# Retention followed by a routed mixture of experts: the due slots of the tail tokens and of the expert weights are changed

## Chip, cores and metric

One NeuronCore of a Trainium2 chip runs the whole kernel. The metric is the device time of one execution in microseconds (us); lower is better. The kernel before has a median of 495.64 us over 14 runs (493.08 to 499.93).

## What is computed

The first half is a decayed attention without softmax: 8 batches, 8 heads, 576 positions, head size 64. Its output, 4608 tokens of 512 numbers, goes to a mixture of 8 experts. Each token takes the two experts with the highest noisy logits and adds their weighted results.

```python
scores = q @ k.T / sqrt(64)
x = (scores * gamma[h] ** (pos_q - pos_k), causal) @ v
logits = x @ w_gate + log1p(exp(x @ w_noise)) * noise
top2, weights = two largest of logits, softmax over the two
out[token] = sum over its two experts e of weight * (relu(x @ w1[e]) @ w2[e])
```

The inputs are float32. The matmuls run in bfloat16.

## The kernel before

**First half: slots.** The attention is cut into 16 units, numbered u = 0 to 15: two batches (a pair, `bp`), four heads (`hq`), one batch of the pair (`b`). A loop over n = 0 to 16 (line 1178) works on them in a software pipeline; one pass of it is called slot n here. The instruction order on each engine is the order of the Python text (`tc.manual_schedule`), so an instruction that has to wait holds everything behind it on its engine. In slot n:

- SyncE (SP) issues the loads of unit n+4: `raw_q`, `raw_k`, `raw_v` (lines 170 and 175), four buffers each. In slots 2, 6 and 10 it also issues the loads of the next tail (line 182).
- TensorE (PE) computes scores of unit n (line 263), the output of unit n-1 (lines 313, 321), transposes q and k of unit n+1 (line 248) and sums states (line 287).
- GpSimd (POOL) casts k and q of unit n+2 with the decay factors: `kn` (line 199), `qb` (line 206).
- ScalarE (ACT) copies out of PSUM and casts: `xT` (327), `QT` and `KT` (250), `vn`, the cast of v of unit n+2 (189), `Tb` (293).
- VectorE (DVE) applies the causal mask to the scores (268).

**Tail tokens.** A unit covers 512 of the 576 positions. The remaining 64 positions of both batches of a pair and all heads are the tail of that pair. `cast_tail(bp)` casts them: q and k on POOL (`qt`, `kt`, line 217), v on ACT (`vt`, line 220). `tr_tail(bp)` transposes `qt` and `kt` on PE (line 229) and copies the result out on ACT (`TT`, line 232). The tail's own scores and output (lines 338 to 357, then `xT`, line 357) come in slots 4bp+2 and 4bp+4. The load buffers `rawt_q`, `rawt_k`, `rawt_v` exist once each. Before, the casts and transposes are placed at the end of these slots:

```python
if u % 4 == 2 and u < 12 or u == 1:
    at.cast_tail((u + 2) // 4)
if u % 4 == 3 and u < 15 or u == 1:
    at.tr_tail((u + 1) // 4)
```

That is: pair 0 cast and transposed in slot 1; pairs 1, 2 and 3 cast in slots 2, 6 and 10 and transposed in slots 3, 7 and 11.

**Router.** When a pair is complete (slots 4, 8, 12, 16) `route(bp)` is appended to a list, and its pieces are issued between the steps of the following slots: logits and rows (`xr`, lines 502 to 507), two table switches on ACT (`nl` 525 and `d` 574), the choice of two experts on DVE, list positions, the placement matrices `olo` and `oh` on DVE (665 to 672), and a store of the rows, `xd<-xr`, on SP (line 653). On POOL it has `pd` (579, 580, 625), `pl` (597 to 648) and the copies into `xr` (651) that the store waits for. In slots 11 to 14 POOL issues the weights of experts 0 and 1 (lines 1096 and 1099).

**Second half: tiles.** The expert stage has 35 tiles of 256 tokens, in order of their expert: two tiles of expert 0, three of expert 1, five of each later one (five more tiles were computed early, between the last slots). PE interleaves g2 of tile i (line 986, the second matmul) with g1 of tile i+1 (line 966, the first matmul, four pieces of 256 rows called fp 0 to 3). ACT takes relu of fp 0 and 2 (971), the copy `xgT` after fp 0 (953) and some of the scaled results `y` (1013); DVE takes relu of fp 1 and 3 (973) and the rest. The piece buffer `p1` has three places.

**Weights of experts 2 to 7.** Each expert has 8 parts of 512 KB. A part is loaded by SP into a staging tile `wst` (lines 902 and 905, four buffers) and cast by ACT into the expert's tile (line 916). Before, a pair of parts is loaded by `wload(i + 1)` at the end of tile i and cast by `wcast(i + 1)` at the end of tile i+1, four tiles for each expert: tiles 0 to 3 for expert 2, 4 to 7 for expert 3, and so on to 20 to 23 for expert 7. Three expert tiles exist, so expert e takes the place of expert e-3. Expert e is used from tile 5e-5.

Of the kernel before, what the change touches and what calls it, by code (L numbers as in the profile page):

```python
# [10 lines left out]
F32 = mybir.dt.float32  # L11
# [4 lines left out]
Act = mybir.ActivationFunctionType  # L16

P = 128
N = 4608
NCOL = N // P  # L20
E = 8
F = 1024
DM = 512
KD = DM // P
KF = F // P
TS = 256
NTE = 5
# [15 lines left out]
LATE = [(e, t) for e in range(E) for t in range(NTE) if (e, t) not in [x[1:] for x in EARLY]]  # L43
# [804 lines left out]
def experts(tc, K, wp, w1, w2, keep, xd, yd, out, W, pre):  # L848

    nc = tc.nc  # L850
# [3 lines left out]
    NT = len(LATE)  # L854
    order = {V.engine, nc.scalar.engine, nc.gpsimd.engine, nc.tensor.engine, nc.sync.engine}
    with tc.tile_pool(name="moe_g", bufs=1) as gp, \
# [14 lines left out]

        st = {}
        writes = []
        parts = {}

        def firsts(i):

# [5 lines left out]
            return [2 * t + s >= ONLYA[e] for s in range(2)]  # L883


        loads = {}
        i0 = -4
        for e in range(2, E):
            i0 = max(i0 + 4, LATE.index((e - 3, NTE - 1)) + 1 if e > 2 else 0)
            for j in range(4):  # L890
                loads[i0 + j] = e, j

        def wload(i):

            if i not in loads:
                return
            e, j = loads[i]
            parts[i] = []
            for k in (2 * j, 2 * j + 1):
                t = stg.tile([P, F], F32, name="wst")  # L900
                if k < KD:
                    nc.sync.dma_start(out=t, in_=w1[e, k * P:(k + 1) * P, :])
                else:
                    f = 2 * (k - KD)
                    nc.sync.dma_start(out=t.rearrange("p (fo d) -> p fo d", fo=2),
                                      in_=w2[e, f * P:(f + 2) * P, :].rearrange("(fo fi) d -> fi fo d", fi=P))
                parts[i].append((k, t))

        def wcast(i):
            if i not in parts:  # L910
                return
            e = loads[i][0]
            if e not in W:
                W[e] = (gp if e % 3 == 2 else wp).tile([P, KD * F + KF * DM], BF16, name=f"w{e % 3}")
            for k, t in parts.pop(i):
                nc.scalar.activation(W[e][:, k * F:(k + 1) * F], t, Act.Copy)  # L916

        def xgof(i):
            return pre[i] if i < len(pre) else xgs[i % NX]
# [120 lines left out]
        with tc.manual_schedule(engines=order):  # L1040
            for i in range(len(pre), 5):
                clear(xgs, i % NX)
                for s in range(2):
                    gather(tc, keep, xd, xgof(i), i, s)
            small(0)
            small(1)
            transp(0)()
            transp(1)()
            for _ in g1(0, {}):
                pass  # L1050
            small(2)
            small(3)
            wload(0)
            pv = 0
            for i in range(NT + 1):
                if i:
                    fin(i - 1)
                if i < NT:
                    ev = transp(i + 2)
                    cb = lambda: comb(i - 1)  # L1060
                    a = g1(i + 1, {0: ev, 1: cb}) if i + 1 < NT else iter(())
                    for _ in g2(i):
                        next(a, None)
                        next(a, None)
                    for _ in a:
                        pass
                    small(i + 4)
                if i + 1 >= NT:
                    comb(i - 1)

                if i + 5 < NT:
                    clear(xgs, (i + 5) % NX)
                for s in range(2):
                    if i + 5 < NT:
                        gather(tc, keep, xd, xgof(i + 5), i + 5, s)
                while pv <= i + 2 and stored(pv, i):
                    for s in range(2):
                        prev(pv, s)
                    pv += 1
                for s in range(2):  # L1080
                    if i and seconds(i - 1)[s]:
                        scat(i - 1, s)
                st.pop(i - 1, None)
                wcast(i)
                wload(i + 1)

        last = nc.gpsimd.tensor_copy(keep["nov2"], keep["nov"]).ins
        for w in writes:
# [15 lines left out]
def kernel(  # L1104
# [12 lines left out]
    nc = tc.nc  # L1117
# [10 lines left out]
    W = {}  # L1128
# [3 lines left out]
    with ExitStack() as actx, tc.manual_schedule(engines=order):  # L1132
        at = Attention(tc, actx, raw, None, q, k, v)
        at.load(0, (nc.scalar, nc.sync, nc.sync))
        for u in (1, 2, 3):
            at.load(u, (nc.sync,) * 3)
        at.load_tail(0, (nc.sync,) * 3)
        at.tables()
        K = at.K = constants(nc, cp)
        wg32 = at.bf.tile([P, KD, 2 * E], F32, name="wg32", bufs=1)  # L1140
        nc.scalar.dma_start(out=wg32[:, :, :E], in_=moe_w_gate.rearrange("(do di) e -> di do e", di=P))
        nc.scalar.dma_start(out=wg32[:, :, E:], in_=moe_w_noise.rearrange("(do di) e -> di do e", di=P))
        wgn = cp.tile([P, KD, 2, 2 * E], BF16, name="wgn")
        rt = Router(tc, actx, K, at, wgn, moe_noise, xd, keep)
        NU = 16
        pend = []
        routed = []

        work = []

        def more():
            while work and next(work[0], work) is work:
                work.pop(0)

        def piece():
            while pend and next(pend[0], pend) is pend:
                pend.pop(0)
                routed.append(0)

        def step():  # L1160
            piece()
            if n == NU:
                more()

        zero = at.cp.tile([P, DM], F32, name="zero")
        nc.gpsimd.memset(zero, 0.0)
        at.cast(0, nc.vector)
        nc.gpsimd.tensor_copy(wgn[:, :, 0], wg32)
        nc.gpsimd.tensor_tensor(wgn[:, :, 1], wg32, wgn[:, :, 0], Alu.subtract)
        at.tr(0, "q")  # L1170
        at.tr(0, "k")
        at.cast_v(0)
        for t in at.Tb:
            nc.vector.memset(t, 0.0)
        at.cast(1, nc.vector)
        at.cast_v(1)
        rt.fixed()
        for n in range(NU + 1):
            u, p = n, n - 1
            live, prev = u < NU, p >= 0  # L1180
            bp, hq, b = at.unit(p)
            tail = prev and b
            if u + 4 < NU:
                at.load(u + 4, (nc.sync,) * 3)
            if n % 4 == 2 and n // 4 < 3:
                at.load_tail(n // 4 + 1, (nc.sync,) * 3)
            if n == 1:
                rt.load_noise(nc.sync)
            if live:
                at.scores(u, 0)  # L1190
            step()
            if prev:
                at.out(p)
            step()
            if u + 1 < NU:
                at.tr(u + 1, "q")
            if n == NU - 2:
                more()
            step()
            if live:  # L1200
                at.scores(u, 1)
            step()
            if u + 2 < NU:
                at.cast(u + 2)
            if u + 1 < NU:
                at.tr(u + 1, "k")
            step()
            if tail:
                at.scores_tail(bp, hq)
            step()  # L1210
            if live:
                at.states(u)
            if tail:
                at.out_tail(bp, hq)
            if prev and p % 4 == 3:
                pend.append(rt.route(bp))
            step()
            if u % 4 == 2 and u < 12 or u == 1:
                at.cast_tail((u + 2) // 4)
            if u % 4 == 3 and u < 15 or u == 1:  # L1220
                at.tr_tail((u + 1) // 4)
            if n in (11, 12, 13, 14):
                load_weights(nc, wp, moe_w1, moe_w2, (n - 11) // 2, W, (n - 11) % 2)
            piece()
            if n == NU - 4:
                nc.sync.dma_start(out=yd[:P, :], in_=zero)

            if n == NU - 3:
                assert len(routed) >= 2
                work.append(early(tc, K, at, keep, xd, yd, W, EARLY, routed))  # L1230
            if n in (NU - 3, NU - 2):
                more()
        while pend:
            piece()
            step()
        rt.finish()

        for i in range(1):
            xg = raw.tile([P, 2, 4, P], F32, name="raw_q").rearrange("p c h w -> p (c h w)")[:, :2 * XW].rearrange(
                "p (s w) -> p s w", s=2)  # L1240
            nc.gpsimd.memset(xg, 0.0)
            for s in range(2):
                gather(tc, keep, xd, xg, i, s)
            pre.append(xg)
        rt.overflow_list()
        while work:
            more()
# [32 lines left out]
```

## Time and profile before

| what | value |
|---|---|
| median of 14 runs | 495.64 us |
| the profiled execution's own time | 496.0 us |
| its span, first to last instruction | 494.0 us |
| slots and early tiles | about 0 to 216 us |
| expert tiles | about 216 to 475 us |
| last scatter, overflow test, end | 475 to 494 us |
| PE busy, whole span | 412.1 us (83%) |
| ACT busy, whole span | 275.7 us (56%) |
| POOL busy, whole span | 274.6 us (56%) |
| DVE busy, whole span | 234.7 us (48%) |
| data moved | 104.18 MB, 211 GB/s on average |

The page divides the span into 40 slices of 12.35 us. A busy share over the whole span mixes the two halves, so it is read by stage. In a timeline row the columns are: start, duration, engine, line, operation, output<-input, shapes, count, and in square brackets the idle time before it with the releaser. SPq and PEq are sequencers: an SPq row is the time in which a DMA was issued, not the transfer itself.

### The profile page before, as it was taken

The page shows a single profiled execution, that of the slowest core. Times are in us where ns is not written, and L with a number is a line of the kernel's source. Part 1 is how long each engine was busy: PE and PEld are TensorE (multiplying, and loading weights), DVE is VectorE, ACT ScalarE, POOL GpSimd, SP SyncE. Part 2 cuts the span into 40 slices and gives each one's busy share as a digit, 9 for nine tenths or more (in the row PEclk, how much of TensorE's full clock was granted, in tenths as well). Part 3 has the DMA queues.
Part 4 walks back from the last instruction along what each step waited for, and adds up shares of the span by engine and source line. Part 5 has one row for each costly group of instructions (what it writes and reads, how often), then busy time and mean ns, then how long its engine had stood idle before and what let it go on. Part 6 is the DMA issues. An engine that isn't in the chain of part 4 may idle for free.

```text
span 494.0 us, 11741 instructions
## 1 busy us (share of the span) xinstructions
PE 412.1 (83%) x4688; PEld 299.9 (61%) x4688; DVE 234.7 (48%) x600; ACT 275.7 (56%) x405; POOL 274.6 (56%) x372
## 2 busy tenths in 40 slices
PE   1675378586877699989999999999999999999950
PEld 1464367464666567666766766666676676766630
DVE  3532066966866738724324434344344454454240
ACT  3681689678658467554665665755654643323200
POOL 5460735835954425585255717547567777776440
PEclk9977597989587799999999999999999999999995
DMA  8999993697795822574697887877978945545330
GB/s 243 285 257 215 269 295 55 205 304 168 205 219 130 173 63 97 175 261 154 217 307 213 278 306 222 317 263 246 349 251 275 343 140 194 169 142 186 112 128 2
DMA packets 92856, 104.18 MB, mean 211 GB/s; under 512 B 22135, under 2 KB 69752, under 8 KB 92800
## 3 DMA queue, kind: packets, MB, share of 16 engines
q1 hardware_dynamic: 77040, 70.04, 47.9%
q0 software_dynamic: 14176, 32.83, 23.3%
q8 instruction: 37, 0.61, 0.5%
q10 hardware_dynamic: 1584, 0.56, 0.4%
q14 instruction: 19, 0.16, 0.1%
HBM read 84.66 MB, written 28.72 MB: 230 GB/s over the span
## 4 chain that ended last, share of the span: by engine, by line
PE 58%; DMA 5%; DVE 4%; ACT 3%; SPq 2%; issue 1%; POOL 1%; POOLq 0%; ACTq 0%
PE p L966 25%; PE po L986 24%; DMA raw_v<-in_v_dram 3%; PE pt L950 3%; PE x L408 1%; SPq L182 1%; PE T L398 1%; PE S L398 1%; DVE olo L665 1%; SPq L175 1%; DVE oh L672 1%; DVE S L268 1%; DVE oh L669 1%; DMA rawt_v<-in_v_dram 1%; ACT xr L505 1%
## 5 line engine op out<-in xcount | busy, mean ns | idle before, releaser
L966 PE MATMUL p<-xgT,w 128*128 128x256 bf16 x1120 | 211.3, 273 | 0.0
L986 PE MATMUL po<-w,hT 128*128 128x512 bf16 x560 | 209.8, 379 | 0.0
L966 PEld LDWEIGHTS <-w 128*128 128x128 bf16 x1120 | 109.6, 98 | 70.3
L973 DVE TENSOR_SCALAR hT<-p 128x512 bf16<-128x512 f32 x70 | 48.4, 692 | 145.5 <-PE p L966 145.5
L971 ACT ACTIVATE hT<-p 128x512 bf16<-128x512 f32 x70 | 41.8, 597 | 119.9 <-PE p L966 94.9
L843 POOL DMA_INDIRECT xg<-xd,xi x68 | 68.9, 1013 | 20.2 <-issue 13.9
L1033 POOL DMA_INDIRECT out_dram<-o,ix x45 | 45.6, 1013 | 58.2 <-DVE o L1027 50.6
L268 DVE TENSOR_TENSOR S<-S,mask 128x1024 bf16<-128x1024 f32 x32 | 39.1, 1221 | 50.6 <-PE S L263 50.6
L995 POOL DMA_INDIRECT prv<-yd,ix x45 | 45.1, 1002 | 25.6 <-DMA yd<-y 12.3
L986 PEld LDWEIGHTS <-hT 128*128 128x128 bf16 x560 | 54.8, 98 | 7.5
L916 ACT ACTIVATE w<-wst 128x1024 bf16<-128x1024 f32 x48 | 47.9, 1048 | 0.0
L953 ACT ACTIVATE xgT<-pt 128x1024 bf16<-128x1024 bf16 x35 | 35.6, 1017 | 1.4 <-PE pt L950 1.4
L199 POOL TENSOR_TENSOR kn<-raw_k,kg 128x1024 bf16<-128x1024 f32 x14 | 26.7, 1904 | 15.0 <-DMA raw_k<-in_k_dram 6.1
L1027 DVE SCALAR_TENSOR_TENSOR o<-po,g,prv 128x512 f32<-128x512 f32 x45 | 31.6, 742 | 0.8 <-PE po L986 0.8
L263 PE MATMUL S<-QT,KT 64*64 64x128 bf16 x512 | 17.2, 269 | 17.5 <-ACT KT L250 8.9
L206 POOL TENSOR_TENSOR qb<-raw_q,qg 128x1024 bf16<-128x1024 f32 x14 | 26.7, 1904 | 0.0
L263 PEld LDWEIGHTS <-KT 64*64 64x64 bf16 x512 | 11.2, 132 | 22.0 <-issue 10.3
L250 ACT ACTIVATE QT<-tr 128x1024 bf16<-128x1024 bf16 x16 | 16.4, 1022 | 12.1 <-DMA raw_v<-in_v_dram 8.1
L293 ACT ACTIVATE Tb<-T 64x512 bf16<-64x512 f32 x32 | 18.9, 590 | 5.8 <-PE T L287 5.3
L950 PE MATMUL pt<-ident,xg 128*128 128x128 bf16 x272 | 20.7, 219 | 1.2 <-ACT xgT L953 1.2
L248 PE MATMUL tr<-ident,qb 128*128 128x128 bf16 x128 | 13.8, 271 | 9.5 <-DVE qb L206 9.5
L287 PE MATMUL T<-vn,kn 64*64 64x64 bf16 (+2 forms) x512 | 21.4, 221 | 0.0
(211 smaller groups left out, 593.2 us busy)
## 6 DMA issues: line engine op xcount, KB each, us to landing
wst<-in_moe_w_dram SPq DMA_DIRECT2D x48, 512.0 KB, 5.8
raw_k<-in_k_dram SPq DMA_DIRECT2D x32, 256.0 KB, 6.3
raw_v<-in_v_dram SPq DMA_DIRECT2D x32, 256.0 KB, 6.5
yd<-y SPq DMA_DIRECT2D x16, 512.0 KB, 3.7
raw_q<-in_q_dram SPq DMA_DIRECT2D x15, 512.0 KB, 6.4
xd<-xr SPq DMA_DIRECT2D x12, 396.0 KB, 4.0
w<-in_moe_w_dram POOLq DMA_DIRECT2D x4, 1024.0 KB, 11.9
yd<-raw_v SPq DMA_DIRECT2D x5, 512.0 KB, 4.0
```

What stands on the lines that cost most here:

```text
L268: nc.vector.tensor_tensor(S.rearrange("p h c r t -> p (h c) (r t)"), p.rearrange("p h (c r) t -> p (h c) (r t)", r=2), self.K["mask"].rear ...
L843: tc.nc.gpsimd.indirect_dma_start(out=xg[:, s, :], out_offset=None, in_=xd[:, :], in_offset=IOff(ap=keep["xi"][:, j:j + 1], axis=0), bound ...
L916: nc.scalar.activation(W[e][:, k * F:(k + 1) * F], t, Act.Copy)
L950: nc.tensor.transpose(pt[:, di, s * P:(s + 1) * P], xb[:, di * P:(di + 1) * P], K["ident"])
L953: return lambda: nc.scalar.activation(xgT, pt, Act.Copy)
L966: nc.tensor.matmul(p1[:, f2, :], lhsT=w[:, o:o + P], rhs=xgT[:, di, :], start=(di == 0), stop=(di == KD - 1))
L971: nc.scalar.activation(hT[:, 2 * fp:2 * fp + 2, :], p1, Act.Relu)
L973: V.tensor_relu(hT[:, 2 * fp:2 * fp + 2, :], p1)
L986: nc.tensor.matmul(po[s], lhsT=hT[:, fi, s * P:(s + 1) * P], rhs=w[:, o:o + DM], start=(fi == 0), stop=(fi == KF - 1))
L995: nc.gpsimd.indirect_dma_start(out=prv[i % NP][:, s, :], out_offset=None, in_=yd[:rows, :], in_offset=IOff(ap=st[i]["ix"][:, s, 1:2], axis=0),
L1027: V.scalar_tensor_tensor(o[:, s, :], st[i]["po"][s], st[i]["g"][:, s:s + 1], prv[i % NP][:, s, :], Alu.mult, Alu.add)
L1033: ins = nc.gpsimd.indirect_dma_start(out=out[:, :], out_offset=IOff(ap=st[i]["ix"][:, s, 0:1], axis=0), in_=st[i]["o"][:, s, :], in_offset ...
```

## The change

Two things are moved; no instruction of the computation is added or taken away.

1. **Tail tokens.** `cast_tail` of pairs 1, 2, 3 moves from the end of slots 2, 6, 10 to the end of slots 4, 8, 12. `tr_tail` moves from slots 3, 7, 11 to slots 5, 9, 13. Pair 0 stays in slot 1. The loads of the tails stay where they are on SP, in slots 2, 6 and 10.
2. **Expert weights.** Parts are now queued one by one. Three are loaded before tile 0; each cast is followed by the load of the next part. Casts are no longer at the end of a tile but inside g1: after fp 0 (behind the `xgT` copy) and after fp 2. Expert 2 still takes two casts in each of tiles 0 to 3. Experts 3 to 7 take 2, 1, 2, 1, 2 casts over five tiles, from tile 5e-11: tiles 4 to 8 for expert 3, up to 24 to 28 for expert 7.

```diff
-        parts = {}
+        parts = []
...
-        loads = {}
-        i0 = -4
+
+        casts = {}
         for e in range(2, E):
-            i0 = max(i0 + 4, LATE.index((e - 3, NTE - 1)) + 1 if e > 2 else 0)
-            for j in range(4):
-                loads[i0 + j] = e, j
-
-        def wload(i):
-
-            if i not in loads:
+            i0 = 5 * e - 11 if e > 2 else 0
+            assert e == 2 or i0 > LATE.index((e - 3, NTE - 1))
+            for j, c in enumerate((2, 1, 2, 1, 2) if e > 2 else (2, 2, 2, 2)):
+                casts[i0 + j] = c
+            assert i0 + j + 1 < LATE.index((e, 0))
+        queue = [(e, k) for e in range(2, E) for k in range(KD + KF // 2)]
+
+        def wload():
+
+            if not queue:
                 return
-            e, j = loads[i]
-            parts[i] = []
-            for k in (2 * j, 2 * j + 1):
-                t = stg.tile([P, F], F32, name="wst")
...
+            e, k = queue.pop(0)
+            t = stg.tile([P, F], F32, name="wst")
...
+            parts.append((e, k, t))
+
+        def wcast(i, j):
+
+            if j >= casts.get(i, 0):
                 return
-            e = loads[i][0]
+            e, k, t = parts.pop(0)
...
-            for k, t in parts.pop(i):
-                nc.scalar.activation(W[e][:, k * F:(k + 1) * F], t, Act.Copy)
+            nc.scalar.activation(W[e][:, k * F:(k + 1) * F], t, Act.Copy)
+            wload()
...
-            wload(0)
+            for _ in range(3):
+                wload()
...
-                    cb = lambda: comb(i - 1)
-                    a = g1(i + 1, {0: ev, 1: cb}) if i + 1 < NT else iter(())
+                    def first():
+                        ev()
+                        wcast(i, 0)
+                    a = g1(i + 1, {0: first, 1: lambda: comb(i - 1), 2: lambda: wcast(i, 1)}) if i + 1 < NT else iter(())
...
-                wcast(i)
-                wload(i + 1)
...
-            if u % 4 == 2 and u < 12 or u == 1:
-                at.cast_tail((u + 2) // 4)
-            if u % 4 == 3 and u < 15 or u == 1:
-                at.tr_tail((u + 1) // 4)
+            if n == 1 or n in (4, 8, 12):
+                at.cast_tail(n // 4)
+            if n % 4 == 1 and n < NU:
+                at.tr_tail(n // 4)
```

More of the change, by code (lines that the diff above doesn't have):

```diff
@@ L883, in seconds @@
             return [2 * t + s >= ONLYA[e] for s in range(2)]
-        loads = {}
-        i0 = -4
+        casts = {}
         for e in range(2, E):
-            i0 = max(i0 + 4, LATE.index((e - 3, NTE - 1)) + 1 if e > 2 else 0)
-            for j in range(4):
-                loads[i0 + j] = e, j
-        def wload(i):
-            if i not in loads:
-                return
-            e, j = loads[i]
-            parts[i] = []
-            for k in (2 * j, 2 * j + 1):
-                t = stg.tile([P, F], F32, name="wst")
[L901 to L910, printed above, removed]
+            i0 = 5 * e - 11 if e > 2 else 0
[6 more added lines that the diff above has]
+            if not queue:
+                return
+            e, k = queue.pop(0)
+            t = stg.tile([P, F], F32, name="wst")
+            if k < KD:
+                nc.sync.dma_start(out=t, in_=w1[e, k * P:(k + 1) * P, :])
+            else:
+                f = 2 * (k - KD)
+                nc.sync.dma_start(out=t.rearrange("p (fo d) -> p fo d", fo=2),
+                                  in_=w2[e, f * P:(f + 2) * P, :].rearrange("(fo fi) d -> fi fo d", fi=P))
+            parts.append((e, k, t))
+        def wcast(i, j):
+            if j >= casts.get(i, 0):
                 return
-            e = loads[i][0]
+            e, k, t = parts.pop(0)
             if e not in W:
                 W[e] = (gp if e % 3 == 2 else wp).tile([P, KD * F + KF * DM], BF16, name=f"w{e % 3}")
-            for k, t in parts.pop(i):
-                nc.scalar.activation(W[e][:, k * F:(k + 1) * F], t, Act.Copy)
+            nc.scalar.activation(W[e][:, k * F:(k + 1) * F], t, Act.Copy)
+            wload()
         def xgof(i):
```

## The prediction

> **What bounds the kernel now.** I read the stages first, then the waits, then the timelines of ACT, PE and SP around the longest wait. The table of stages (columns: PE, PEld, DVE, ACT, POOL busy us with counts, granted PE clock, DMA share, GB/s):
>
> ```profile
> 37.00:54.00 17.00, 6.78 (x150) 5.39 (x145) 2.67 (x3) 2.08 (x5) 3.46 (x4) 0.67 1.05 213
> 54.00:77.00 23.00, 16.55 (x370) 13.77 (x370) 11.04 (x27) 21.43 (x30) 11.27 (x9) 0.72 1.11 278
> 77.00:90.00 13.00, 9.90 (x213) 8.05 (x210) 9.65 (x27) 10.79 (x17) 8.95 (x19) 0.87 0.11 22
> ...
> 216.00:475.00 259.00, 257.77 (x1955) 179.57 (x1955) 111.89 (x296) 133.40 (x178) 157.05 (x158) 1.00 0.70 235
> ```
>
> The expert stage is PE alone: 257.77 of 259 us busy at full clock. Nothing off PE shortens it. The slots (0 to 216) have holes: from 37 to 54 ACT did 2.08 us of work. The list of waits (us in total, times, longest) names the cause:
>
> ```profile
> ACT vt L220 <- DMA rawt_v<-in_v_dram: 17.7, 3, 14.6
> ...
> POOL qt L217 <- DMA rawt_q<-in_q_dram: 13.5, 2, 13.2
> ...
> PE tr L229 <- ACT QT L250: 12.0, 1, 12.0
> ```
>
> and the timelines show it in place, ACT first, then PE, then SP:
>
> ```profile
> 38.87 0.38 ACT L357 ACTIVATE xT<-x 128x256 bf16<-128x256 f32 x1
> 53.85 0.63 ACT L220 ACTIVATE vt<-rawt_v 128x512 bf16<-128x512 f32 x1 [14.59 <-DMA rawt_v<-in_v_dram]
> 54.38 1.07 ACT L327 ACTIVATE xT<-x 128x512 bf16<-128x512 f32 x2
> ```
>
> ```profile
> 43.15 1.25 PE L287 MATMUL T<-vn,kn 128*64 128x192 bf16 x32
> 56.41 0.26 PE L229 MATMUL tr<-ident,qt 128*128 128x128 bf16 x1 [12.02 <-ACT QT L250]
> ```
>
> ```profile
> 47.84 1.47 SPq L182 DMA_DIRECT2D rawt_v<-in_v_dram  x2
> ...
> 74.59 1.99 SPq L182 DMA_DIRECT2D rawt_v<-in_v_dram  x2
> 89.61 1.62 SPq L653 DMA_DIRECT2D xd<-xr  x3
> ```
>
> Slot 2 issues the tail of pair 1 on SP and asks for its cast in the same slot. SP issues it at 44 to 49.3, ACT wants it at 39.25, it lands at 53.85. Nobody needs `vt` before slot 6. PE runs slot 3 to 44.4 and then stands until 56.41 behind ACT's `QT`. The last two SP rows show the second effect: loads run without a gap to 76.6, then SP waits 13 us for the router's `xr`; between 77 and 90 the DMA share is 0.11.
>
> **Tail, slot 2 to 4.** Without `vt` ACT can go on at 39.25, but `xT` needs PE's output of unit 2, which ends at 40.22 + 0.82 = 41.04. From the start of `xT` to the end of `KT` slot 3 took 54.38 to 58.22, 3.84 us. `vn` in it needs `raw_v` of unit 5, issued by 36.4 (half of it earlier); with the page's 6.5 us to landing this is about 42.5, in time. So `KT` ends near 41.1 + 3.84 = 44.9, not 58.22: **13.3 us earlier**. PE's scores of slot 4 waited for that `KT` ([0.85 <- ACT KT] at 58.28), so slot 4 moves with it.
>
> What is late next? Slot 4's casts. The load of unit 6 was issued at 40.6 to 44; `rawt_q`, issued behind it, was there at 50.67, so unit 6 is there by about 50; `vn` is due at 62.33 - 13.3 = 49.0. That may cost 0 to 1, mostly taken up because `KT` there waits for PE anyway. Then `vt`, now at the end of slot 4: due behind the slot's `xT` (66.39 - 13.3 = 53.1), landed at 53.85: a wait of 0.75, and 0.53 to the next start. The next, `xr`, was at 67.16, but waited 0.76 for PE; it goes from due 53.9 to 54.4. **12.7 us are left.** POOL: `kn`, `qb` of unit 6 from about 48.5 to 52.2, `qt` and `kt` to 54.3; its next casts were due at 64.84 - 12.7 = 52.1 but wait for unit 7, issued 50.2 to 53.7, to about 58 to 60. `qb` of 7 is first used in slot 6 (77.02 - 12.7 = 64.3): covered. `vn` of 7: due 71.98 - 12.7 = 59.3, lands 52.7 + 6.5 = 59.2: no margin, 0 to 1 us. Unit 8 lands near 65, due at 67.5 and later; from there the load keeps ahead, since a unit takes some 6 us on SP and a slot 7 to 10 us.
>
> **Transposes, slots 5, 9, 13.** ACT gets `TT`, 1.02 us (1024 ns in the tile's rows), right behind `Tb` and ahead of the table switch and `d`, with 8 transposes (0.9 us) on PE beside it. `d` leads to DVE's `df`, for which POOL's `pl` waits 2.65 us at 78.80: on the path. I charge 1.0 us each, 3.0 in all (bounds 0 and 1.9, ACT and PE one after the other). What leaves slots 3, 7, 11 gives nothing: `xT` at 60.23 was due with PE's output anyway, at 92.54 PE waits 1.45 us for DVE's `S`, at 130.61 ACT waits 0.47 us for PE.
>
> **Casts, slots 6, 10 to 8, 12.** POOL loses 2 x 1.04 us ahead of `xr` and `xd`, ACT 0.63 us and in slot 10 a wait of 2.06 us. Slot 7 and slot 11 are paced by DVE (PE waits 2.66 and 3.14 us for `S` L268), so ACT's part there is worth nothing; below 2.7 us if I misread it. POOL's 2.08 us lets SP store `xd` and load unit 15 earlier. That load landed 16.7 us after its issue beside the weights of expert 0, and `vn` waited 2.40 us for it at 148.03: **2.1 us gained** (0 to 2.4). The 2.08 us that slots 8 and 12 take on POOL fall into its waits of 2.59 us (`raw_k`, at 100.31) and 4.64 us (at 140.48). Without that cover: 2.1 each.
>
> **SP.** `rawt` has one buffer, so the loads of slots 6 and 10 wait for casts two slots later than before. Slot 6: SP comes at 70.4, the cast ends near 54.4. Slot 10: SP comes near 100, `kt` of pair 2 ends near 99.8 - 12 = 88. Margins of 16 and 12 us; no wait. The `xd` store of pair 0 waits for `xr` at 89.38 - 12 - 2 = 75: when SP gets there at 76.6 it is ready, and unit 11 is issued 13 us earlier, as much as its use moves.
>
> **Expert stage.** 48 casts of 1.05 us remain. Tiles follow each other by 7.39 us (transposes at 229.32, 236.72, 244.11 in the chain):
>
> ```profile
> 308.95 0.60 ACT L971 ACTIVATE hT<-p 128x512 bf16<-128x512 f32 x1 [1.91 <-PE p L966]
> 309.45 1.99 ACT L916 ACTIVATE w<-wst 128x1024 bf16<-128x1024 f32 x2
> 311.34 0.68 ACT L1013 ACTIVATE y<-po,g 128x512 f32<-128x512 f32 x1
> 312.92 0.60 ACT L971 ACTIVATE hT<-p 128x512 bf16<-128x512 f32 x1 [0.90 <-ACT y L1013]
> 313.42 1.02 ACT L953 ACTIVATE xgT<-pt 128x1024 bf16<-128x1024 bf16 x1
> ```
>
> The cast after fp 0 fits into the 1.91 us idle before the second relu; the one after fp 2 is where a pair was. Loads are issued three casts ahead, 1.5 tiles or 11 us at least; they land in 3.8 to 9.6 us. Cost and gain: 0.
>
> **Sum.** 12.7 - 3.0 + 2.1 = 11.8 us. The profiled execution took 496.0 us, its span of 494.0 and 2.0 around it that nothing here touches: 496.0 - 11.8 = 484.2. It lay 0.4 above the median of 495.64, which gives 483.8. I say **484.0**.
>
> **A rule weighed.** PE ran this stretch cold: 16 scores took 0.64 us from 41.8 to 63, 0.42 us from 67 on. The Trainium skill, "TensorE: Matmul & The Clock Gate", What's actually happening, says that an idle window of 3.4 us throttles the clock to half and a busy one releases it. By it, removing a 12 us gap would keep PE warm and halve some 5 us of PE work in slot 4, an estimate of 2.5 us more, 481.5. The trace speaks against counting on it: slots 1 and 2 (22 to 36 us), with no such gap, show 0.64 us too. I add nothing and keep 2.5 us for the low end.
>
> **Rivals.**
> - *The loads take the place of the tail* (0.17): 37 to 77 already runs at a DMA share over 1, so the gained time ends in waits for units 7 to 11. For it: no margin at `vn` of 7. Against: the hole of 77 to 90, which is there to be filled. If the backlog delays unit 11 by 3 to 5 us, 7 to 9 us are left: 487 to 489; at worst nearer 493.
> - *More than I count* (0.14): `TT` hidden in all three slots (+3.0) and a warmer PE (+2.5): up to 17.3 us, 478 to 481.
> - *The wait only changes its slot, no gain* (0.05): if ACT's stand was hidden behind the loads' pace. PE's 12.02 us and the SP hole speak against it. 493 to 498.
> - *Slower: casts inside g1* (0.04). ACT is in order: a cast that waits for its part holds the relu of fp 2 behind it. That relu has 0.8 us spare, and PE goes on until piece buffer three is needed, about 3.3 us more. From a landing time of 11 + 4.1 = 15 us on, PE stalls; at 16 us some 0.9 us in each of about 20 tiles with two casts, 18 us: 484 + 18 = 502. The longest landing in this stage is 9.6 us, and the new order spreads the load thinner.
>
> **Numbers.** The forecast, 481 to 487, has 0.60. Faster by over 0.5% (about what a measurement of this kernel can tell from no change, 2.5 us) is 0.60 + 0.17 + 0.14 = 0.91, same 0.05, slower 0.04. The range 479 to 489 takes in the warm PE and most of the first rival, 0.81 together.
>
> **What would show it.** Right: no ACT wait for `rawt_v` over 1 us; `TT` of pair 1 in slot 5; the stage 77 to 90 filled with loads; first tile's g1 near 206.5 instead of 218.4; tile pace still 7.39 us. Wrong: waits of `vn` or `kn` for `raw_v`, `raw_k` of units 6 to 11; `xd` late on SP; ACT idle ahead of `w` L916.

## The result, and the profile after

| | before | after |
|---|---|---|
| median (runs) | 496.75 us (47) | 485.96 us (10) |
| lowest to highest | 491.83 to 500.55 us | 485.42 to 489.25 us |
| profiled execution, its span | 496.0 us, 494.0 us | 489.64 us, 487.5 us |

The ratio is 0.9802 [0.9772, 0.9831], which is 9.8 us less at 496.75 us (8.4 to 11.3 by the interval). The medians lie 10.8 us apart. A ratio here leaves out the executions in which the chip was in its slower state, so it can differ from the quotient of two medians, most of all on the third chip used below. The profiled execution of after is longer than any of the ten in the table; its span is 6.5 us shorter than that of before. So the stages are read from it, and the size from the ratio.

The table of stages of after, with the same columns as before (the granted PE clock is the share of full speed that PE was allowed):

```profile
37.00:54.00 17.00, 13.92 (x325) 11.08 (x327) 5.66 (x6) 13.06 (x20) 9.57 (x7) 0.80 0.95 203
54.00:77.00 23.00, 17.71 (x364) 14.57 (x353) 18.70 (x48) 18.94 (x28) 11.18 (x18) 0.78 1.09 283
77.00:90.00 13.00, 7.89 (x168) 6.54 (x169) 10.84 (x13) 7.95 (x10) 10.56 (x13) 0.74 1.06 292
...
216.00:475.00 259.00, 253.81 (x1904) 175.29 (x1902) 111.03 (x296) 131.38 (x173) 153.82 (x154) 1.00 0.68 227
```

From 37 to 54 us ACT now works 13.06 us, where it was 2.08, and PE 13.92, where it was 6.78. The hole of 77 to 90 is full of loads: DMA share 1.06, where it was 0.11. The last row is still PE alone: 253.81 us, less than before because the tiles now end at 469.8 instead of 476.3, and no wait of PE for another engine is listed from 216 us on.

ACT's timeline from slot 4 to slot 5 of after:

```profile
52.76 0.38 ACT L357 ACTIVATE xT<-x 128x256 bf16<-128x256 f32 x1
54.57 0.63 ACT L220 ACTIVATE vt<-rawt_v 128x512 bf16<-128x512 f32 x1 [1.43 <-DMA rawt_v<-in_v_dram]
55.10 1.01 ACT L505 ACTIVATE xr<-tr 128x1024 bf16<-128x1024 bf16 x1
...
64.14 1.02 ACT L232 ACTIVATE TT<-tr 128x1024 bf16<-128x1024 bf16 x1
65.18 1.28 ACT L574 ACT_TABLE_LOAD   x1
66.47 0.21 ACT L574 ACTIVATE d<-d 128x9 f32<-128x9 f32 x1
```

The tail's cast still ends a wait for its load, but of 1.43 us instead of 14.59, and slot 5 starts with `xr` at 55.10 instead of 67.16. `TT` stands ahead of the table switch and `d`. SP's timeline of after shows the store that used to be issued at 89.61:

```profile
75.04 2.11 SPq L182 DMA_DIRECT2D rawt_v<-in_v_dram  x2
77.54 1.69 SPq L653 DMA_DIRECT2D xd<-xr  x3
79.28 1.19 SPq L170 DMA_DIRECT2D raw_q<-in_q_dram  x1
```

SP no longer waits for `xr` here. What is late instead stands in the list of waits of after (total, times, longest):

```profile
POOL kn L199 <- DMA raw_k<-in_k_dram: 14.0, 4, 4.2
...
ACT vn L189 <- DMA raw_v<-in_v_dram: 3.5, 4, 1.5
...
ACT vt L220 <- DMA rawt_v<-in_v_dram: 2.5, 2, 1.4
```

Before, the tail's cast had 17.7 us, and the other two

```profile
POOL kn L199 <- DMA raw_k<-in_k_dram: 6.1, 2, 3.5
...
ACT vn L189 <- DMA raw_v<-in_v_dram: 3.9, 2, 2.4
```

Part of the wait for loads went from the tail's cast to `kn`.

In the expert stage the tiles still follow each other by 7.39 us (`pt` at 252.24, 259.63, 267.02). One tile of it on ACT, and the group of the weight casts on the page of after:

```profile
262.06 0.60 ACT L973 ACTIVATE hT<-p 128x512 bf16<-128x512 f32 x1 [1.76 <-PE p L968]
262.56 1.02 ACT L955 ACTIVATE xgT<-pt 128x1024 bf16<-128x1024 bf16 x1
263.46 1.06 ACT L917 ACTIVATE w<-wst 128x1024 bf16<-128x1024 f32 x1
265.49 0.60 ACT L973 ACTIVATE hT<-p 128x512 bf16<-128x512 f32 x1 [0.97 <-PE p L968]
265.98 1.05 ACT L917 ACTIVATE w<-wst 128x1024 bf16<-128x1024 f32 x1
```

```profile
L917 ACT ACTIVATE w<-wst 128x1024 bf16<-128x1024 f32 x48 | 50.6, 1054 | 0.0
```

The number behind the second bar is the idle time ahead of the group: 0.0 us over 48 casts. No cast waited for its part, and behind the casts shown the relu still waits for PE, not PE for it.

**Where the gain stands.** The same instruction in the traces, at its start. The last column is a second execution of the same kernel, `after_again` of the experiments, whose slots can be compared:

| instruction | before | after | shift | after_again | shift |
|---|---|---|---|---|---|
| `xr`, first of slot 5 | 67.16 | 55.10 | -12.1 | 55.09 | -12.1 |
| `vn` of unit 7 | 71.98 | 60.16 | -11.8 | 60.09 | -11.9 |
| `d`, slot 5 | 77.24 | 66.47 | -10.8 | 66.40 | -10.8 |
| `vn` of unit 10 | 97.45 | 87.93 | -9.5 | 87.84 | -9.6 |
| `vn` of unit 11 | 108.12 | 99.91 | -8.2 | 98.08 | -10.0 |
| `d`, slot 9 | 113.38 | 106.22 | -7.2 | 104.38 | -9.0 |
| `vn` of unit 14 | 134.30 | 127.14 | -7.2 | 125.31 | -9.0 |
| `vn` of unit 15 | 148.03 | 138.36 | -9.7 | 136.52 | -11.5 |
| `d`, slot 13 | 153.30 | 144.66 | -8.6 | 143.12 | -10.2 |
| `xgT` of the first expert tile | 216.76 | 208.66 | -8.1 | 207.52 | -9.2 |
| first 32 matmuls of its g1 take | 3.66 | 4.89 | | 3.66 | |

The gain is complete at the start of slot 5. After that it is paid away in small pieces, and one piece comes back at unit 15. The column of before is one execution. `weights_only` of the experiments, whose slots are ordered as before, has `d` of slot 5 at 79.31, `vn` of unit 10 at 100.00 and the first tile at 219.40, which is 2.1 to 2.6 us later. So a piece of 1 us lies within what two executions of the same slots differ by. The two executions of the same kernel part between units 10 and 11, by 1.8 us. PE's timeline of after shows there

```profile
89.80 1.91 PE L287 MATMUL T<-vn,kn 128*64 128x192 bf16 x32
...
94.43 0.64 PE L263 MATMUL S<-QT,KT 64*64 64x128 bf16 x16
```

and that of `after_again`

```profile
89.60 1.25 PE L287 MATMUL T<-vn,kn 128*64 128x192 bf16 x32
...
93.15 0.42 PE L263 MATMUL S<-QT,KT 64*64 64x128 bf16 x16
```

The same matmuls, half as long again; PE's granted clock is 0.81 from 90 to 108 us in the one and 0.91 in the other. The first tile's transposes and g1 are slow in the same way (1.01 and 4.89 us, where before and `after_again` have 0.61 and 3.66), which is the 1.6 us between the 8.1 us at the first tile and the 6.5 us of the span. With these 1.6 and 1.8 us back, the 6.5 us of the profiled execution would be 9.9, close to the 9.8 of the ratio.

### The profile page after: what moved, and what is told of

It reads as the page before. It is cut to its first block, busy times and chain, and to the rows that moved or that the text cites. A ratio compares the mean times of both kernels' runs of the same rounds, so it can differ in the third digit from the quotient of the medians.

```text
span 487.5 us, 11760 instructions
## 1 busy us (share of the span) xinstructions
PE 420.1 (86%) x4688; PEld 305.3 (63%) x4688; DVE 237.7 (49%) x600; ACT 276.5 (57%) x405; POOL 274.5 (56%) x372
## 4 chain that ended last, share of the span: by engine, by line
PE 51%; issue 5%; DVE 4%; POOL 4%; ACT 3%; DMA 1%; POOLq 0%; ACTq 0%
PE p L968 22%; PE po L988 21%; PE pt L952 3%; PE x L408 2%; POOL out_dram L1035 2%; PE T L398 1%; POOL prv L997 1%; PE S L398 1%; DVE olo L665 1%; DVE oh L672 1%; DMA prv<-yd,ix 1%; DVE oh L669 1%; ACT xr L505 1%; DMA out_dram<-o,ix 1%; ACT L574 0%
## 5 line engine op out<-in xcount | busy, mean ns | idle before, releaser
L973 ACT ACTIVATE hT<-p 128x512 bf16<-128x512 f32 x70 | 41.8, 597 | 114.8 <-PE p L968 82.9
L917 ACT ACTIVATE w<-wst 128x1024 bf16<-128x1024 f32 x48 | 50.6, 1054 | 0.0
L263 PE MATMUL S<-QT,KT 64*64 64x128 bf16 x512 | 17.5, 272 | 12.7 <-DVE S L268 7.1
L327 ACT ACTIVATE xT<-x 128x512 bf16<-128x512 f32 x32 | 17.3, 592 | 13.1 <-PE x L321 13.1
L287 PE MATMUL T<-vn,kn 64*64 64x64 bf16 (+2 forms) x512 | 24.2, 237 | 0.0
## 6 DMA issues: line engine op xcount, KB each, us to landing
w<-in_moe_w_dram POOLq DMA_DIRECT2D x4, 1024.0 KB, 11.3
```

The costliest lines, as they stand in the source:

```text
L263: nc.tensor.matmul(p[e * HD:(e + 1) * HD, h, 2 * c + r, :], lhsT=d["K"][s, hp, c, r, e, :], rhs=d["Q"][s, hp, 2 * c + e, :], start=(c == 0 ...
L973: nc.scalar.activation(hT[:, 2 * fp:2 * fp + 2, :], p1, Act.Relu)
```

## Experiments

My theory: one wait, that of pair 1 in slot 2, is the whole gain; pairs 2 and 3 and the weights are near nothing; three `TT` cost 3 us. Rivals: the weights' new order has a part in it; the pace of the loads, not `TT`, takes what is lost of the 13 us; or two DVE operations that stood behind POOL do. The runs came from three chips. On the second and third the expert stage of the kernels traced there takes some 33 to 52 us more (first to last `xgT`, 279 us in `after_again` instead of 246 in after), with many pauses of PE that the profile puts down to no other engine, while the slots take the same time. So there only ratios on one chip, and rows from the slots, are compared.

### Halves of the change

`tail_only` is before with only the last part of the diff, `weights_only` before with all but that part.

> The tail's casts and transposes are moved as in the changed kernel, the weights come as before. If the whole effect is in the slots, this gives the changed kernel's time within 1 us, 485 to 487. If the weights part carries some of it, this is slower than the changed kernel by that amount, over 1.5 us.

> Only the weights come part by part over five tiles, the tail is as before. If PE alone bounds the expert stage, the time is that of the kernel before within 0.5%, the tile pace stays 7.39 us. If casts inside g1 hold relu back, it is slower by more than 2 us and PE shows waits on ACT in the tiles; if the pairs of casts had cost something, it is faster by more than 2 us.

Measured beside the same runs of before (median 496.66 us): `tail_only` 485.38 us, ratio 0.9783 [0.9735, 0.9831]; `weights_only` 495.51 us, 0.9973 [0.9941, 1.0004]. The tails are the whole effect. By its interval the weights' order saves at most 3 us and costs at most 0.2, and no effect of it is measured.

### Pairs of the tail

`pair1_only` and `pairs23_only` are before with these lines in place of the old four:

```diff
# pair1_only
+            if n in (1, 4, 6, 10):
+                at.cast_tail((n + 2) // 4)
+            if n in (1, 5, 7, 11):
+                at.tr_tail({1: 0, 5: 1, 7: 2, 11: 3}[n])
# pairs23_only
+            if n in (1, 2, 8, 12):
+                at.cast_tail({1: 0, 2: 1, 8: 2, 12: 3}[n])
+            if n in (1, 3, 9, 13):
+                at.tr_tail({1: 0, 3: 1, 9: 2, 13: 3}[n])
```

> Only pair 1 is cast in slot 4 and transposed in slot 5, pairs 2 and 3 and the weights are as before. My theory: the wait of 14.6 us is the whole gain, 12 us less 1 for the copy TT in slot 5: 10 to 12 us below the kernel before, a little better than the full change, since two TT copies stay where they are hidden. Rival, that pairs 2 and 3 carry a good part (their waits of 2.1 us and POOL's 2.1 us): 3 us or more slower than the full change.

> Pair 1 stays in slots 2 and 3, pairs 2 and 3 are cast in slots 8 and 12 and transposed in 9 and 13; weights as before. My sum: minus 2.1 for unit 15 and plus 2 x 1.0 for TT: no change, within 1 us. If the TT copies are hidden: 2 us faster. If they cost ACT and PE one after the other: 2 us slower.

Measured: `pair1_only` 488.2 us, 0.9823 [0.9777, 0.9868]; `pairs23_only` 497.66 us, 1.0017 [0.9981, 1.0053]. Pair 1 is nearly all of it: 8.8 us by the ratio, where I had expected 10 to 12 and a little more than the full change gives, which did not come. A wait is left in this kernel, as ACT's timeline of `pair1_only` in slot 6 shows:

```profile
73.51 0.38 ACT L357 ACTIVATE xT<-x 128x256 bf16<-128x256 f32 x1
80.95 0.63 ACT L220 ACTIVATE vt<-rawt_v 128x512 bf16<-128x512 f32 x1 [7.05 <-DMA rawt_v<-in_v_dram]
```

With slots 12 us earlier, pair 2's cast in its old slot now meets its load on the way, and waits 7.05 us. Before, that row (84.05 us) has no wait. So moving pairs 2 and 3 is worth nothing alone, and keeps this wait away once pair 1 is cured. That this saves time is not shown: the intervals of `pair1_only` and `tail_only` overlap, and its first tile came at 207.47 us, as early as in the other cures.

### What takes the rest: TT, or DVE behind POOL

The trace of after holds something that the prediction did not count. DVE's and POOL's timelines in slot 5 of after:

```profile
58.84 1.68 DVE L548 TENSOR_TENSOR nl<-nl,noise 128x64 f32<-128x64 f32 x1 [0.67 <-ACT nl L525]
60.45 1.88 DVE L549 TENSOR_TENSOR nl<-nl,noiset 128x8 f32<-128x8 f32 x1
62.36 0.23 DVE L550 TENSOR_TENSOR nl<-nl,lg 128x72 f32<-128x72 f32 x1
```

```profile
58.54 1.90 POOL L199 TENSOR_TENSOR kn<-raw_k,kg 128x1024 bf16<-128x1024 f32 x1 [4.22 <-DMA raw_k<-in_k_dram]
60.40 1.90 POOL L206 TENSOR_TENSOR qb<-raw_q,qg 128x1024 bf16<-128x1024 f32 x1
```

Before, with POOL idle beside them, the first two were

```profile
71.21 0.23 DVE L548 TENSOR_TENSOR nl<-nl,noise 128x64 f32<-128x64 f32 x1 [0.44 <-ACT nl L525]
71.35 0.16 DVE L549 TENSOR_TENSOR nl<-nl,noiset 128x8 f32<-128x8 f32 x1
```

Now `kn` waits for its load and falls on them, and each DVE operation ends when POOL's does (60.44 and 60.52, 62.30 and 62.33). That is 3.2 us more on DVE ahead of `d`. The Trainium skill, "SBUF — State Buffer", SBUF: two separate sides, names a lock: a DVE operation with two SBUF inputs and a GpSimd operation that reads SBUF exclude each other for a whole instruction. Three kernels tell the two suspects apart, each an edit of after:

```diff
# tt_late: TT behind the unit's output, one slot later
+            if n in (6, 10, 14):
+                at.tr_tail(n // 4)
...
-            if n % 4 == 1 and n < NU:
-                at.tr_tail(n // 4)
+            if n == 1:
+                at.tr_tail(0)
# nl_psum: one of the two inputs lies in PSUM
-        nl = sp.tile([P, C, E], F32, name="nl")
+        nl = self.bank[:, :C * E].rearrange("p (c e) -> p c e", c=C)
# both: the two edits together
```

> The changed kernel with the transposes of pairs 1 to 3 moved on to slots 6, 10 and 14, behind the output of the unit before and ahead of the tail's scores. My theory: TT ahead of the table switch and d cost 1.0 us in each of slots 5, 9 and 13, so up to 3 us come back; in slot 5 only 0.4, because there DVE's two products with the noise took 3.6 us instead of 0.4 and d waits for them as well. 483 to 484. Rival, that TT was hidden and the missing 2 us are the clock's: no change within 0.7 us.

> The changed kernel with the router's tile nl in PSUM instead of SBUF, so that DVE's products with the noise have one input there. If their 1.7 and 1.9 us in slot 5 come from two SBUF inputs beside POOL's cast of unit 7, they go back to 0.4 us or less each. The time stays nearly the same by itself, within 0.5 us, because TT and the table switch on ACT hold d as long. If the slow products were the whole missing piece: 2 to 3 us faster.

> Both edits together. If TT and the slow products hold d side by side in slot 5, taking both gives 1 us there and 1 each in slots 9 and 13: 3 us below the changed kernel, and more than the sum of the two alone.

Measured on the second chip (before: 548.41 us): `tt_late` 539.24 us, 0.9816 [0.9751, 0.9881]; `nl_psum` 535.81 us, 0.9777 [0.9721, 0.9834]; `both` 538.31 us, 0.9821 [0.977, 0.9873]. DVE's timeline of `nl_psum`, and the POOL cast beside it:

```profile
58.57 0.23 DVE L548 TENSOR_TENSOR R<-R,noise 128x64 f32<-128x64 f32 x1 [0.60 <-ACT R L525]
58.84 0.17 DVE L549 TENSOR_TENSOR R<-R,noiset 128x8 f32<-128x8 f32 x1
...
59.93 1.79 DVE L543 TENSOR_TENSOR scr<-scr,desc 128x72 f32<-128x72 f32 x1
```

```profile
59.73 1.90 POOL L206 TENSOR_TENSOR qb<-raw_q,qg 128x1024 bf16<-128x1024 f32 x1
```

The trace agrees with the lock: with one input in PSUM the two operations take 0.23 and 0.17 us beside POOL's cast of `kn` (57.87 to 59.77), and the next operation with two SBUF inputs, L543, takes over the wait until POOL's `qb` ends (59.73 + 1.90). But it is not on the path: in slot 5 DVE had its `d` ready at 64.29 (64.12 + 0.17), and ACT ran its own `d` only at 65.97, behind `TT` and the table switch. `tt_late` alone meets the other side: ACT's `d` then waits 0.62 us for DVE's. With `both`, `d` of slots 5, 9 and 13 comes at 64.39, 103.24 and 141.53, which is 1.1 to 2.0 us earlier than in `after_again` (2.1 to 3.1 than in after). At the end of the slots 0.8 of it is left against `after_again` (1.9 against after):

| kernel | `xgT` of the first expert tile, us |
|---|---|
| before, weights_only, pairs23_only | 216.76, 219.40, 218.13 |
| after, tail_only, pair1_only | 208.66, 206.36, 207.47 |
| tt_late, nl_psum, both | 207.40, 207.84, 206.72 |
| after_again, nl_psum_2, lead1, stage1, early_tail | 207.52, 206.82, 205.27, 207.13, 207.47 |

Every cure of pair 1's wait ends its slots at 205 to 209 us, whatever else was edited, and every kernel without one at 217 to 219. The 3 us for `TT` are there at `d`, but a kernel that spares `d` that time does not measurably end earlier. My expectations for `tt_late` and `both`, which reckoned with 3 us, are missed.

Both after and `nl_psum` were run again on the third chip (before: 541.34 us):

> The changed kernel once more, unaltered, beside the next three on one chip. 0.98 of the kernel before. In slot 5 DVE's two products with the noise take 1 to 2 us each again, if that belongs to the kernel and not to one execution.

> The changed kernel with nl in PSUM, on the same chip as the changed kernel. In the run before, the products fell to 0.23 and 0.17 us and the next operation with two SBUF inputs took 1.79 us in their stead: d was ready 1.8 us earlier and ACT's table switch and TT held it. So within 0.5 us of the changed kernel; 1.5 us or more faster only if DVE's chain was the longer one.

`after_again` 525.79 us, 0.983 [0.9733, 0.9928]; L548 and L549 took 1.61 and 1.88 us again, and its slots are the last column of the ledger. `nl_psum_2` 529.42 us, 0.9699 [0.948, 0.9917]: its interval covers both theories, so it decides nothing on time; 0.22 and 0.17 us repeat the lock.

### How far the weights are from the edge

`lead1` is after with one part loaded ahead instead of three; `stage1` takes away three of the four staging buffers as well.

```diff
# lead1 and stage1
-            for _ in range(3):
+            for _ in range(1):
# stage1 alone
-         tc.tile_pool(name="moe_w", bufs=4) as stg, \
+         tc.tile_pool(name="moe_w", bufs=1) as stg, \
```

> The changed kernel with one part of the weights loaded ahead instead of three. A part is asked for after the cast before it, so a cast comes every 5.1 to 5.8 us of landing plus 1.05, 6.5 us, while the plan has one every 4.6 us: the rival of the prediction (relu held behind a cast that waits) is made to happen. 8 casts of an expert then take 52 us and not 37: PE should wait for ACT, some 10 us and more per expert, 520 us or over. If ACT's order had slack for this, the time would stay within 3 us.

> The changed kernel with one staging buffer for the weights and one part ahead. Four buffers let SP run ahead whatever the order of the text; with one, a part is loaded only after the cast before it, so a cast comes every 5.1 + 0.5 + 1.05 us = 6.6 us at best. 8 casts take 53 us where five tiles take 37: PE waits for ACT, 16 us for each of five experts and some 20 in the first tiles, 560 to 590 us. If relu had slack for casts that wait, under 500 us.

`lead1`: 534.71 us in its one run, beside 548.41 for before; a single run can't tell it from the other cures. It is not slower, which is a miss. ACT waited 7.7 us for `wst` in 6 casts. SP's timeline tells why it was not more: three parts were issued from 202.27 us on, ahead of the first cast at 214.06, although the program asks for one. ACT's casts do not hold SP while a buffer is free; after them SP only issues stores of results (`yd`, at 204.55 and 220.80) until 221.22. So the order in the program is not the lead in time. `stage1`: 537.55 us, 1.0005 [0.9938, 1.0073], against 0.983 for `after_again` on the same chip. That is 11.8 us by the medians, and the gain of the tails is gone. Its list of waits, and then the waits of PE in its expert stage:

```profile
ACT w L917 <- DMA wst<-in_moe_w_dram: 80.8, 35, 4.3
```

```profile
PE p L968 <- ACT hT L973: 8.6, 7, 2.7
PE pt L952 <- ACT xgT L955: 2.8, 1, 2.8
PE p L968 <- ACT w L917: 1.2, 1, 1.2
```

In `after_again` PE waited 0.3 us for ACT in that stage; here it is 8.6 + 2.8 + 1.2 = 12.6 us, which fits the 11.8. It is not the whole difference of the two traces: these are the shortest execution of `after_again` and the longest of `stage1`, 18.4 us apart, and PE's matmuls of the stage add up to 9 us more in `stage1`. ACT's timeline of `stage1` shows the mechanism:

```profile
304.88 0.58 ACT L973 ACTIVATE hT<-p 128x512 bf16<-128x512 f32 x1
308.88 1.06 ACT L917 ACTIVATE w<-wst 128x1024 bf16<-128x1024 f32 x1 [3.42 <-DMA wst<-in_moe_w_dram]
309.84 0.58 ACT L973 ACTIVATE hT<-p 128x512 bf16<-128x512 f32 x1
```

The cast waits 3.42 us for its part, and the relu behind it starts at once, with PE's output lying ready. 80.8 us of waiting cost about 12, because most of it takes the place of waits that the relus had anyway: the idle time of ACT ahead of L973 falls from 147.2 us in `after_again` to 86.7. What the three places of `p1` do for this was not varied. I had expected 560 us or more, some 75 above after; 12 came.

### Another cure of the same wait

`early_tail` leaves all casts where before has them, and loads pair 1's tail in slot 0 instead of slot 2:

```diff
-            t = self.raw.tile([P, 8, HD], F32, name=f"rawt_{n}", bufs=1)
+            t = self.raw.tile([P, 8, HD], F32, name=f"rawt_{n}", bufs=2)
...
-            if n % 4 == 2 and n // 4 < 3:
-                at.load_tail(n // 4 + 1, (nc.sync,) * 3)
+            if n in (0, 6, 10):
+                at.load_tail({0: 1, 6: 2, 10: 3}[n], (nc.sync,) * 3)
```

> The kernel before, but the tail of pair 1 is loaded in slot 0 into a second buffer instead of in slot 2; casts and transposes stay in slots 2 and 3. The wait for vt goes without moving vt. Theory, loads set the pace from 30 to 77 us: the 2.6 us of tail go ahead of units 5 and 6, vn in slot 3 waits some 5 us for its load, and 7 to 9 us are gained of the 13. Rival, that only the place of the wait in ACT's order counted: 12 to 13 us gained.

Measured: 531.81 us, 0.9899 [0.976, 1.0038]; by its interval anything from no gain to that of after. The slots say more. ACT's timeline of `early_tail`:

```profile
40.66 0.63 ACT L220 ACTIVATE vt<-rawt_v 128x512 bf16<-128x512 f32 x1 [1.05 <-DMA rawt_v<-in_v_dram]
...
45.91 1.06 ACT L189 ACTIVATE vn<-raw_v 128x1024 bf16<-128x1024 f32 x1 [2.73 <-DMA raw_v<-in_v_dram]
...
54.04 1.06 ACT L189 ACTIVATE vn<-raw_v 128x1024 bf16<-128x1024 f32 x1 [1.99 <-DMA raw_v<-in_v_dram]
...
79.93 0.63 ACT L220 ACTIVATE vt<-rawt_v 128x512 bf16<-128x512 f32 x1 [4.18 <-DMA rawt_v<-in_v_dram]
```

The tail is there in time, but loads that it was put ahead of are late: `vn` of units 5 and 6 wait 2.73 and 1.99 us, which is the 5 us expected, and pair 2's cast, in its old slot 6, waits 4.18. `d` of slot 5 comes at 69.28, 8.0 us earlier than before, not 10.8; I had expected 7 to 9. Yet the first tile's `xgT` comes at 207.47. The pace of the loads does take a part of the 13 us, and further on that part is swallowed too.

## Why the prediction was right, step by step

- **Tail, slots 2 to 4: right.** Counted -12.7, measured -12.1 at `xr` of slot 5 in both executions. `vt` ended its wait at 54.57 and not at the 53.85 that I took over from before; its wait of 1.43 us is over the 1 us that I had set as a sign. `pair1_only` and `pairs23_only` show that this wait alone carries the gain.
- **Transposes, slots 5, 9, 13: right in size.** Counted 1.0 each. From the `vn` ahead to `d` the ledger has +1.0, +1.0, +1.1 in after and +1.1, +1.0, +1.3 in `after_again`. `pair1_only` has this 1.0 in slot 5 alone (59.74 to 66.05, where before has 71.98 to 77.24), and `pairs23_only` in slots 9 and 13 alone. That they reach the end, as "on the path" says, is not shown: `tt_late` and `both` bring `d` forward and end no earlier beyond the scatter.
- **Casts in slots 8 and 12, and the load of unit 15: right.** Counted -2.1, measured -2.5 between `vn` of units 14 and 15; its wait of 2.40 us is gone. `pairs23_only`, in which pair 1 stays, has the same step: 11.2 us between the two, 13.7 before. A wait of SP for the `rawt` buffers did not come.
- **Nothing for slots 6 to 9 and for the end of the slots: 2 too much against the profiled before, and not settled.** In `after_again` 1.2 us are lost between `d` of slot 5 and `vn` of unit 10 (0.4 come back by unit 11), and 1.0 between `d` of slot 13 and the first tile. For these stretches I had no term in the sum. With the 0.6 of the first step this is most of what lies between 11.8 and 9.2. After loses 1.8 us more by the clock. What takes the 1.2 and the 1.0 is not settled; `nl_psum` only shows that DVE's wait in slot 5 does not set ACT's `d` there. Against the slots of `weights_only`, whose traced execution is the longest of its twelve, the two losses are 0.8 and 0.7, and the first tile of `after_again` comes 11.9 us earlier, close to the sum that I counted. So these losses may be differences between executions.
- **Expert stage, 0: right.** `weights_only` is 0.9973 [0.9941, 1.0004], the pace 7.39 us. The reason was in part wrong: I said loads are issued three casts ahead; `lead1`, in its one run, shows that this lead is not what keeps the parts in time; with three of the four buffers gone as well, `stage1` loses the gain.
- **The rule weighed.** PE was warmer where the gap had been, and counting nothing fits what came: 37 to 54 went from a granted clock of 0.67 to 0.80, 77 to 90 from 0.87 to 0.74, 108 to 124 from 1.00 to 0.58. The same holds over the kernels. Without a cure (before, `weights_only`, `pairs23_only`) 54 to 77 has 0.57 to 0.72 and 77 to 90 has 0.87 to 0.99; with one (nine kernels, eleven executions) 0.76 to 0.93 and 0.50 to 0.74. The work in a stretch is then some 10 us further on, so this is no comparison of like with like; but the warmth of the first stretch did not last. Nor could it bring slot 5 forward, whose `xr` stands behind `vt` and its load. My reading of the cold stretch left out that 16 scores took 0.42 us at 38.22 in before, ahead of the gap. And the rule as I quoted it does not foretell the clock here: in after the granted clock is 0.50 from 85 to 95 us, although the longest pause of PE from 73 us on is the 2.00 us at 82.35.
- **Rivals.** *The loads take the place*: seen only in part. `kn` waits for loads more, but before 60 us, where the gain was still whole; in slots 6 to 9 none of its waits in after is for a load. So a sign that I had listed for being wrong came (3.95 and 4.22 us for units 6 and 7) without the loss that it stood for. `early_tail` shows what this rival would have cost: 2.8 us at `d` of slot 5, and nothing at the end. *More than I count*: not seen in the time. *The wait only changes its slot*: seen as `pair1_only`'s 7.05 us, without its price. *Slower*: `stage1` shows its mechanism, at 12 us, where I put 18.

The sum of 11.8 us stands against 9.8 by the ratio, just outside its upper end of 11.3, and inside the 8.4 to 13.2 of `tail_only`. The mechanism held: one wait of ACT carries the gain. The total does not test the two smaller terms, since -3.0 and +2.1 nearly cancel; only the rows above do. One sign came out otherwise: the first tile's g1 starts at 210.54 us in after and 209.04 in `after_again`, not near 206.5.

Open: why all cures end the slots at 205 to 209 us. A shift of up to 3 us at `d` is gone there, and the scatter is as wide as the effects looked for. Whether the chain of slots 14 to 16 or the clock takes it was not told apart. That pairs 2 and 3 must move too is not shown by the time either.

## What to carry to other kernels

An in-order engine that asks for data in the slot that orders it stops everything behind it: put the use where the data will be, and look at who else falls idle to size the gain, here PE for 12 us and SP for 13. Then follow one instruction per slot through both traces, since a gain that is whole at one place is paid away later at others, and a cost on the path of one slot need not be on the path of the end. A lead written in the program means little while the number of buffers lets the issuing queue run ahead.

## What the hardware showed that I had not expected

- A DVE operation of 0.16 us with two SBUF inputs took 1.88 us beside a POOL cast, ending with it. With one input in PSUM it took 0.17 us beside such a cast (`nl_psum`, `nl_psum_2`).
- PE's work of one kind takes different times, by the granted clock: 32 `T` matmuls 1.25 or 1.91 us, and the first 32 matmuls of the first tile's g1 3.66 us in `after_again` and 4.89 in after, where 205 to 216 us had a clock of 0.84 in place of 1.00. Two executions of one kernel differ by 2 to 3 us in the slots and this tile, for the most part by that, which is more than most of the edits tried here are worth.
- The expert stage takes some 33 to 52 us more on two of three chips, with waits of PE named "issue" and waits of ACT and DVE with a remote releaser, while the slots agree. The cause is not known.
